# A Fourier filter and a cosine-gated layer on one core: the transforms' inputs split 18 and 20 slots ahead, the filters' rows loaded at the split

## The chip, the cores and the metric

One core of a Trainium2 chip runs the whole computation in one launch. The metric is the device time of that launch in microseconds; lower is better. Several executions of one kernel give a median, and one further execution is recorded by the profiler.

## What is computed

Eight sequences of 3008 tokens with 256 features are filtered in the frequency domain along the sequence; each of the 24064 resulting tokens then goes through two matrix products with a cosine gate between them. Everything is float32.

```python
X = np.fft.rfft(x, axis=1)
y = np.fft.irfft(X * (filt_r + 1j * filt_i)[None], n=3008, axis=1)   # x: 8 x 3008 x 256
h = y.reshape(24064, 256) @ w_in                                     # 256 x 2048
out = (h * np.cos(h)) @ w_out                                        # 2048 x 256
```

## The kernel before

**Split products.** Single precision is kept by writing an operand as a high and a low part in a type that TensorE multiplies at full rate, and by adding three products (high by high, low by high, high by low). A "split" of an operand is thus two instructions: a cast on ACT (the high part) and a subtraction on POOL (the low part). Both are in-order engines, so a split stands in a row with the other work of ACT and POOL.

**The layer.** The tokens are cut into 31 chunks (`SIZES`: 470, 464, then 510 tokens) and a tail that is computed another way. A chunk goes through eight steps, one for each pair of 128-wide blocks of the hidden layer. A step is `hidden` (L698, 12 products on TensorE, "PE" from here on, into `hp`) and the gate: ACT rounds (L708), DVE takes the rest (L709), ACT takes the sine (L712), DVE multiplies (L713), ACT casts to `gh` (L718), POOL subtracts to `gl` (L719). `project` (L733, 12 products that read `gh` and `gl`) follows two steps later (`LAG = 2`).

**The transforms.** Sequence 0 is transformed ahead of the layer. Sequences b = 1 to 7 are transformed underneath it, each as one block of small items strewn between the layer's products: first 16 items of `stage1(b, i)`, then 12 of `stage23(b, i)`. All transformed sequences go through DRAM tensors (`z1`, `z2`) between the stages, and `stage4` brings them back as tokens for later chunks (L543 loads, L555 products).

- `stage1`, b > 1: loads `xf` (L327, issued on SP), splits it into `xh` for each of two halves (L357 on ACT, L358 on POOL, which subtracts in place so that one product carries both parts), multiplies twice (L363), copies out on DVE (L365) and stores (L367, SP).
- `stage23`: loads the filter rows `f` (L375, L376, SP) and the two halves `zf`, `zg` of what stage 1 stored (L385, SP); adds the halves on POOL (L389); splits the sum into `zh` and `zl` (L393 on ACT, L394 on POOL); multiplies three times (L286, L287 read `zh`, L288 reads `zl`); DVE multiplies by the filter rows (L404, L405) and adds (L406); a second split (L409, L410) and three more products follow.

The products of b = 1 in stage 1 need no split, as they run in plain float32 (L336).

**The written order.** Time in the program is counted in slots: 64 slots are 470 tokens of the layer (a step of a 510-token chunk is 8.7 slots). Each part of an item has a due slot, and `run_due` writes the parts between the layer's products when their slot has come. With t for the slot of an item's first product:

```python
step = (end - start - GAP12) / (ones + 2 * n23)
t = start + step * (i - SOON + 1 if b == 1 else 2 * i + 1)
plan(stage1(b, i), t - AHEAD1, [t, t + step][: b], split=t - SPLIT1 if b > 1 else None)
t = start + step * (ones + 2 * i + 2) + GAP12
plan(stage23(b, i), t - AHEAD2, [t, t + GAP23], lambda b=b: len(wrote1.get(b, ())) == 2 * n1, t - SPLIT2)
```

So loads are written `AHEAD` slots ahead of the product and splits `SPLIT` slots ahead. For b > 1, `end - start` is 260 slots, `ones` is 32 and `n23` is 12: an item comes every 2 x (260 - 20) / 56 = 8.57 slots.

From chunk 1 on, PE runs exactly in the written order (`manual_schedule`); ACT, DVE, POOL and the DMA queue of SP are ordered by a scheduler that places instructions by a simulated timeline, with the written order as priority. In chunk 0 the scheduler orders PE too.

**Buffers.** `xh`, `zh` and `zl` share two sets of three buffers (`sh`, `sl`), `f` has three, `xf` three (with the weights' raw tiles), `zf` shares five with the loads of `stage4` (`ld`), and the transforms' products share two banks of PSUM (`ps`).

Of the kernel before, what the change touches and what calls it, by code (L numbers as in the profile page):

```python
# [10 lines left out]
F32 = mybir.dt.float32  # L11
# [10 lines left out]
P = 128  # L22
# [9 lines left out]
APART = 3  # L32
FIRST, LENGTH, BETWEEN = 80, 260, 24
BEFORE, LATER = 140, 28
GAP12, GAP23 = 20, 24
AHEAD1, AHEAD2, AHEAD4 = 28, 28, 24
SPLIT1, SPLIT2 = 10, 12
HALF, WIDE = 252, 512
SIZES = [470] * 4 + [464] + [510] * 26
FROM4, APART4, LATE4, CLOSE4 = 12, 20, 2, 14  # L40
# [137 lines left out]
def fft_filter_then_cos_glu(ctx: ExitStack, tc: tile.TileContext, ins, outT):  # L178
    nc = tc.nc
    x, fa, fb, sgn = ins["x"], ins["fa"], ins["fb"], ins["sgn"]  # L180

    const = ctx.enter_context(tc.tile_pool(name="const", bufs=1))
    fft = ctx.enter_context(tc.tile_pool(name="fft", bufs=2))
# [15 lines left out]
    @contextmanager  # L199
    def behind():  # L200

        if hold:
            with tc.issue_after(hold[0]):
                yield
        else:
            yield

    def load_mats(*names):
        for i, name in enumerate(names):
            rows, cols = ins[name].shape[0], ins[name].shape[1] // 2  # L210
            if i % 2 == 0:
                two = fft.tile([P, 2, 512], F32, name="mats", tag="f", bufs=3)
            raw = two[:, i % 2]
            with tc.issue_after(last_x[0]):
                nc.sync.dma_start(raw[:rows, : 2 * cols], ins[name])
            m = const.tile([P, 2 * cols], F32R, name=name, tag=name)[:rows]
            nc.scalar.copy(m, raw[:rows, : 2 * cols])
            mats[name] = m if name == "m1" else (m[:, :cols], m[:, cols:])
# [65 lines left out]
    def mm3(out, m, hi, lo):  # L284

        nc.tensor.matmul(out, m[0], hi, start=True, stop=False)  # L286
        nc.tensor.matmul(out, m[1], hi, start=False, stop=False)  # L287
        nc.tensor.matmul(out, m[0], lo, start=False, stop=True)  # L288
# [7 lines left out]
    def psum_f(b):  # L296
        if b == 0 and len(done) < 2:
            if not spare:
                spare.extend(ps_h.tile([P, 2, 512], F32, name="hp")[:, u] for u in range(2))
                spare.append(ps_f.tile([P, 512], F32, name="ps", tag="ps"))  # L300
            return spare.pop(0)
        return ps_f.tile([P, 512], F32, name="ps", tag="ps")


    last_x = []
# [63 lines left out]

    def stage23(b, i):  # L370
        piece = slice(i * 512, (i + 1) * 512)
        f = fft.tile([P, 2, 512], F32, name="f", bufs=3)
        fbt, fat = f[:, 0], f[:, 1]
        with tc.issue_after(last_x[0]) if b == 1 else behind():
            nc.sync.dma_start(fbt, fb[:, piece])  # L375
            nc.sync.dma_start(fat, fa[:, piece])  # L376
        zf = fft.tile([P, 512], F32, name="zf", tag="ld", bufs=5)
        assert len(wrote1[b]) == 2 * n1
        if b == 1:
            nc.sync.dma_start(zf, z1s[b].rearrange("n (c k) d -> (n c) (k d)", c=2)[:, piece])  # L380
        else:
            zg = wprep.tile([P, 512], F32, name="zg", tag="t", bufs=5)
            for v, to in enumerate((zf, zg)):
                of = z1s[b].rearrange("n (c v k) d -> (n c) v (k d)", c=2, v=2)[:, v, piece]
                nc.sync.dma_start(to, of)  # L385
        yield
        if b > 1:
            with tc.issue_after(hold[3]):
                nc.gpsimd.tensor_tensor(zf, zf, zg, ALU.add)  # L389
        hi = fft.tile([P, 512], F32R, name="zh", tag="sh", bufs=3)  # L390
        lo = fft.tile([P, 512], F32R, name="zl", tag="sl", bufs=3)
        with tc.issue_after(hold[1]):
            nc.scalar.copy(hi, zf)  # L393
        nc.gpsimd.tensor_tensor(lo, zf, hi.bitcast(F32), ALU.subtract)  # L394
        yield
        ps = psum_f(b)
        mm3(ps, mats["m2"], hi, lo)
        sw = fft.tile([P, 512], F32, name="sw", bufs=2)
        ya = fft.tile([P, 512], F32, name="ya", bufs=2)
        for k in range(2):  # L400
            ks = slice(k * D, (k + 1) * D)
            kc = NK + 2 * i + k
            for to, of in ((slice(0, 64), slice(64, P)), (slice(64, P), slice(0, 64))):
                nc.vector.scalar_tensor_tensor(sw[to, ks], ps[of, ks], sg[of, kc : kc + 1], fbt[of, ks], ALU.mult, ALU.mult)  # L404
        nc.vector.tensor_tensor(ps, ps, fat, ALU.mult)  # L405
        nc.vector.tensor_tensor(ya, ps, sw, ALU.add)  # L406
        yh = fft.tile([P, 512], F32R, name="yh", bufs=2)
        yl = fft.tile([P, 512], F32R, name="yl", bufs=2)
        nc.scalar.copy(yh, ya)  # L409
        nc.gpsimd.tensor_tensor(yl, ya, yh.bitcast(F32), ALU.subtract)  # L410
        yield
        ps = psum_f(b)
        if i == 0:
            mm3(ps[:, :D], mats["m30"], yh[:, :D], yl[:, :D])
            mm3(ps[:, D:], mats["m3"], yh[:, D:], yl[:, D:])
        else:
            mm3(ps, mats["m3"], yh, yl)
        z = fft.tile([P, 512], F32, name="z2t", tag="st", bufs=4)
        nc.scalar.copy(z, ps)
        wrote2.setdefault(b, []).append(i)  # L420
        nc.scalar.dma_start(z2[b * NJ : (b + 1) * NJ].rearrange("j (h c k) d -> (j h c) (k d)", h=2, c=2)[:, piece], z)
# [266 lines left out]
    def hidden(c, s):  # L688
        nt = SIZES[c]
        yh, yl = ys[c]  # L690
        assert filled[c] == nt, (c, filled)
        hp = ps_h.tile([P, 2, 512], F32, name="hp")
        for u in range(2):
            fs = slice(u * P, (u + 1) * P)
            for t in range(NDT):
                for n, (w, y) in enumerate(((0, yh), (0, yl), (1, yh))):
                    with tc.issue_after(last_h[0]) if c == s == 0 else nullcontext():
                        mm = nc.tensor.matmul(hp[:, u, :nt], w_in[s][w][:, t, fs], y[:, t, :nt],  # L698
                                              start=(t == 0 and n == 0), stop=(t == NDT - 1 and n == 2))
                if u == 0 or t == 0:  # L700
                    yield
        last_h[:] = [mm.ins]
        with tc.high_priority() if c == 0 else nullcontext():
            gs[c, s] = gate(hp[:, :, :nt], nt, nc.vector if c == 0 else nc.gpsimd)
# [256 lines left out]
    def convert(g=None, behind=None):  # L961
        with tc.issue_after((behind or hold)[1]), tc.issue_after((behind or hold)[2]):
            if g is None:
                g = prep.pop(0)(None)
                next(g)
            next(g, None)
# [47 lines left out]
    def slot(token):  # L1014
        return SLOTS * NS * token / RUN
# [56 lines left out]
    for k in range(len(steps)):  # L1072
        parts = []
        if k == 2:
            for g in soon[2:]:
                next(g, None)
        if k == 1:
            for g, tie in zip(raws, first_gate):
                convert(g, tie)
        c, s = steps[k]  # L1080
        now_at[0] = c
        if (c, s) == (1, 0):
            fixed.enter_context(tc.manual_schedule(engines={mybir.EngineType.PE}))
        if k < len(steps):
            if s == 6 and c == 0:
                for g in soon:
                    next(g, None)
            if s == 0 and c == 2:
                load_mats("m2", "m3", "m30")
            if s == 0 and c == 3:  # L1090
                load_mats("m1")
            if c == 0:
                while prep and len(prep) > 2 * (NS - 1 - s) - JUST_W:
                    convert()
            parts.append(hidden(c, s))
        if k >= LAG and k < len(steps) - 1:
            parts.append(project(*steps[k - LAG]))
        rate = SIZES[c] / RUN
        now = slot(begins[c]) + SLOTS * rate * s
        for g in parts:  # L1100
            for _ in range(SLOTS // 2):
                run_due(now)
                next(g, None)
                now += rate
# [93 lines left out]
```

## Time and profile before

| what | value |
|---|---|
| median of 3 runs | 2584.69 us (2584.17 to 2585.67) |
| profiled execution | 2588.62 us, its span 2586.8 us |
| PE matmul busy | 2431.1 us, 94% of the span |
| POOL, ACT, DVE busy | 70%, 64%, 63% of the span |
| mean granted TensorE clock | 0.979 |
| moved by DMA | 277.5 MB, mean 107 GB/s |

The profiled execution is 3.9 us above the median and inside one launch, so sums below are made against 2588.62 us. The blocks of the transforms lie between about 195 us and 1820 us of the span; what follows is the tail. "Idle before" is the time in which an engine had nothing running ahead of an instruction, and "waited for" names the instruction of another engine that ended that time. The granted clock is a share of 2.4 GHz; it has two levels, 1.2 and 2.4 GHz, so that a mean of 0.96 over a stretch stands for 8% of it at the lower one.

### The profile page before, as it was taken

Reading aid. Unit: us, or ns where it says so; the run is one execution under the profiler, and the core shown is the slowest. Engines: PE = TensorE matmul, PEld = TensorE weight load, DVE = VectorE, ACT = ScalarE, POOL = GpSimd, SP = SyncE. Lnnn points to the kernel's source line nnn. Section 1 sums busy time; section 2 is a strip of 40 time slices with the busy share of each in tenths; the row PEclk is TensorE's granted clock in tenths of the full one; section 3 lists DMA queues with packets and bytes.
Section 4 is the critical chain, followed back from the end, with each engine's and each line's share of the span. In section 5 each row is a group of like instructions: output and inputs, shape, how many; then the busy total and the mean of one; then the engine's idle time right before and its main releaser. Section 6 shows DMA issues by size and latency. Waiting matters only on the chain. (4 is left out here: it accounts for less than half of the span.)

```text
span 2586.8 us, 35103 instructions
## 1 busy us (share of the span) xinstructions
PE 2431.1 (94%) x12127; PEld 2019.4 (78%) x12127; DVE 1642.0 (63%) x2328; ACT 1663.1 (64%) x2469; POOL 1818.2 (70%) x1465
## 2 busy tenths in 40 slices
PE   7899988999899989999989999889999999999999
PEld 3788866777777768777768777667899999999998
DVE  4836644666566557556745666565577777777776
ACT  4866655667556656665656666555677777777776
POOL 3786666768677768676767777675677777777775
PEclk9999999999999999999989999999999999999999
DMA  8663343544443445445435444343000000000000
GB/s 294 203 210 101 106 129 106 163 136 141 140 145 122 127 130 166 121 118 166 146 103 150 158 134 129 106 149 113 28 20 28 24 28 21 28 20 29 20 17 17
DMA packets 187432, 277.52 MB, mean 107 GB/s; under 512 B 19344, under 2 KB 102480, under 8 KB 187256
## 3 DMA queue, kind: packets, MB, share of 16 engines
q1 hardware_dynamic: 155448, 223.11, 28.8%
q10 hardware_dynamic: 31808, 52.18, 5.6%
q8 instruction: 97, 1.59, 0.3%
q14 instruction: 79, 0.65, 0.1%
HBM read 177.16 MB, written 98.06 MB: 106 GB/s over the span
## 5 line engine op out<-in xcount | busy, mean ns | idle before, releaser
L719 POOL TENSOR_TENSOR gl<-g,gh 128x1020 fp32r<-128x1020 f32 (+2 forms) x240 | 569.1, 2371 | 371.3 <-ACT gh L718 197.6
L698 PE MATMUL hp<-y,w_in 128*128 128x510 f32 (+2 forms) x2976 | 763.7, 397 | 4.3 <-DVE g L713 3.6
L698 PEld LDWEIGHTS hp<-y,w_in 128*128 128x128 f32 x2976 | 575.0, 194 | 128.8 <-issue 7.0
L733 PE MATMUL acc<-gh,w_out 128*128 128x510 f32 (+2 forms) x1984 | 627.1, 398 | 0.0
L709 DVE TENSOR_TENSOR g<-g,hp 128x1020 f32<-128x1020 int32 (+2 forms) x248 | 298.0, 1202 | 272.2 <-ACT g L708 268.1
L733 PEld LDWEIGHTS acc<-gh,w_out 128*128 128x128 f32 x1984 | 374.9, 192 | 77.5 <-issue 3.3
L712 ACT ACTIVATE g<-g,half_pi 128x1020 f32<-128x1020 f32 (+2 forms) x248 | 282.4, 1139 | 187.2 <-DVE g L709 182.8
L733 PE MATMUL acc<-gl,w_out 128*128 128x510 f32 (+2 forms) x992 | 390.4, 395 | 3.1 <-DVE gl L719 2.6
L713 DVE TENSOR_TENSOR g<-g,hp 128x1020 f32<-128x1020 f32 (+2 forms) x248 | 297.5, 1200 | 138.2 <-ACT g L712 136.7
L718 ACT CAST gh<-g 128x1020 fp32r<-128x1020 f32 (+2 forms) x248 | 256.6, 1035 | 173.3 <-DVE g L713 171.9
L708 ACT ACTIVATE g<-hp 128x1020 int32<-128x1020 f32 (+2 forms) x248 | 250.3, 1009 | 159.8 <-PE hp L698 149.6
L358 POOL TENSOR_TENSOR xh<-xf,xh 48x512 fp32r<-48x512 f32 x192 | 243.1, 1285 | 0.0
L404 DVE SCALAR_TENSOR_TENSOR sw<-ps,sg,f 64x256 f32<-64x256 f32 x336 | 162.4, 483 | 120.4 <-PE ps L288 115.8
L761 ACT ACTIVATE qg<-qg,half_pi 128x496 f32<-128x496 f32 (+1 forms) x272 | 187.5, 711 | 70.3 <-DVE qg L760 70.1
L365 DVE COPY z1t<-ps 96x512 f32<-96x512 f32 x192 | 131.6, 685 | 155.6 <-PE ps L363 150.5
L733 PEld LDWEIGHTS acc<-gl,w_out 128*128 128x128 f32 x992 | 190.4, 192 | 44.0 <-DVE gl L719 3.4
L863 PE MATMUL acc<-hg,w_out 128*128 128x496 f32 (+1 forms) x548 | 183.8, 390 | 0.0
L863 PE MATMUL acc<-hgh,w_out 128*128 128x496 f32 (+1 forms) x544 | 182.9, 390 | 0.6 <-POOL hgh L841 0.6
L863 PE MATMUL acc<-hgl,w_out 128*128 128x496 f32 (+1 forms) x540 | 181.3, 390 | 0.0
L410 POOL TENSOR_TENSOR yl<-ya,yh 128x512 fp32r<-128x512 f32 x84 | 108.8, 1296 | 47.6 <-ACT yh L409 47.5
L394 POOL TENSOR_TENSOR zl<-zf,zh 128x512 fp32r<-128x512 f32 x84 | 108.2, 1290 | 40.4 <-ACT zh L393 40.4
L363 PE MATMUL ps<-xh,m 96*96 96x512 f32 x192 | 80.7, 420 | 58.5 <-POOL xh L358 58.1
(162 smaller groups left out, 4193.8 us busy)
## 6 DMA issues: line engine op xcount, KB each, us to landing
xf<-in_x SPq DMA_DIRECT2D x224, 192.0 KB
z<-z1t SPq DMA_DIRECT2D x192, 192.0 KB
z<-z SPq DMA_DIRECT2D x98, 240.0 KB
f<-in_fb SPq DMA_DIRECT2D x84, 256.0 KB
f<-in_fa SPq DMA_DIRECT2D x84, 256.0 KB
zf<-z SPq DMA_DIRECT2D x84, 256.0 KB
z<-z2t ACTq DMA_DIRECT2D x84, 256.0 KB
zg<-z SPq DMA_DIRECT2D x72, 256.0 KB
```

The source lines that it names most:

```text
L358: nc.gpsimd.tensor_tensor(xh[:Q], xf[:Q, v], xh[:Q].bitcast(F32), ALU.subtract)
L404: nc.vector.scalar_tensor_tensor(sw[to, ks], ps[of, ks], sg[of, kc : kc + 1], fbt[of, ks], ALU.mult, ALU.mult)
L698: mm = nc.tensor.matmul(hp[:, u, :nt], w_in[s][w][:, t, fs], y[:, t, :nt], start=(t == 0 and n == 0), stop=(t == NDT - 1 and n == 2))
L708: rounded = nc.scalar.activation(g.bitcast(I32), h, AF.Copy, bias=0.25)
L709: rest = nc.vector.tensor_tensor(g, g.bitcast(I32), h, ALU.subtract)
L712: sine = nc.scalar.activation(g, g, AF.Sin, bias=half_pi, scale=-TWO_PI)
L713: mult = nc.vector.tensor_tensor(g, g, h, ALU.mult)
L718: cast = nc.scalar.copy(gh, g)
L719: lower = engine.tensor_tensor(gl, g, gh.bitcast(F32), ALU.subtract)
L733: nc.tensor.matmul(acc, w_out[s][w][:, u, es], g[:, u], start=(s == 0 and u == 0 and n == 0), stop=(s == NFT // 2 - 1 and u == 1 and n == 2))
L761: nc.scalar.activation(g, g, AF.Sin, bias=half_pi, scale=-TWO_PI)
L863: nc.tensor.matmul(acc, w[a][:, u, e * P : (e + 1) * P], b[:, :, p], start=(q, u, p, n) == (0, 1, 0, 0), stop=(end and p == 1 and n == 2))
```

## The change

The splits of stage 1 are written 18 slots ahead of the first product instead of 10, those of stages 2 and 3 20 slots instead of 12; the loads of `xf` move from 28 to 34 slots ahead, those of `zf` and `zg` from 28 to 36. The gap between the two stages of a block grows from 20 to 28 slots at the same length of a block, so the items come every 8.29 slots instead of 8.57. The loads of the filter rows `f` move from the item's first part (28 slots ahead) to the part with the split (20 slots ahead). PE's written order begins with chunk 2 instead of chunk 1, so the scheduler orders chunk 1 as it does chunk 0.

```diff
-GAP12, GAP23 = 20, 24
-AHEAD1, AHEAD2, AHEAD4 = 28, 28, 24
-SPLIT1, SPLIT2 = 10, 12
+GAP12, GAP23 = 28, 24
+AHEAD1, AHEAD2, AHEAD4 = 34, 36, 24
+SPLIT1, SPLIT2 = 18, 20
...
     def stage23(b, i):
         piece = slice(i * 512, (i + 1) * 512)
-        f = fft.tile([P, 2, 512], F32, name="f", bufs=3)
-        fbt, fat = f[:, 0], f[:, 1]
-        with tc.issue_after(last_x[0]) if b == 1 else behind():
-            nc.sync.dma_start(fbt, fb[:, piece])
-            nc.sync.dma_start(fat, fa[:, piece])
         zf = fft.tile([P, 512], F32, name="zf", tag="ld", bufs=5)
...
         yield
+        f = fft.tile([P, 2, 512], F32, name="f", bufs=3)
+        fbt, fat = f[:, 0], f[:, 1]
+        with tc.issue_after(last_x[0]) if b == 1 else behind():
+            nc.sync.dma_start(fbt, fb[:, piece])
+            nc.sync.dma_start(fat, fa[:, piece])
         if b > 1:
...
-        if (c, s) == (1, 0):
+        if (c, s) == (2, 0):
             fixed.enter_context(tc.manual_schedule(engines={mybir.EngineType.PE}))
```

How this moves instructions is shown at two places.

First, stage 1 of b = 5, item 12, on POOL and on PE. `xh_9625` and `xh_9628` are the two halves that the item's products read, `gl_9616` the gate's low part that stands ahead of them. POOL before, then PE before:

```order
L719 TENSOR_TENSOR gl_9558<-g_9552,gh_9557 128x2x510
L358 TENSOR_TENSOR xh_9575<-xf_9449,xh_9575 48x512
L358 TENSOR_TENSOR xh_9578<-xf_9449,xh_9578 48x512
L719 TENSOR_TENSOR gl_9616<-g_9610,gh_9615 128x2x510
L358 TENSOR_TENSOR xh_9625<-xf_9502,xh_9625 48x512
L358 TENSOR_TENSOR xh_9628<-xf_9502,xh_9628 48x512
```

```order
L698 MATMUL hp_9707<-y0_8840,w_in0_7_94 128x510
L698 MATMUL hp_9707<-y1_8841,w_in0_7_94 128x510
L698 MATMUL hp_9707<-y0_8840,w_in1_7_95 128x510
L363 MATMUL ps_9734<-xh_9628,m1_1919 96x512
L733 MATMUL acc0_9444<-gh_9615,w_out0_5_106 128x510
L733 MATMUL acc0_9444<-gh_9615,w_out1_5_107 128x510
L733 MATMUL acc0_9444<-gl_9616,w_out0_5_106 128x510
```

On POOL `gl_9616` is made ahead of both halves; on PE the products of both halves come ahead of the first product that reads `gl_9616` (that of `xh_9625` 13 rows ahead of it, that of `xh_9628` the 3 rows shown).

The same item now, with `gl_9511` as the gate's part that stands ahead on POOL. POOL now, then PE now:

```order
L719 TENSOR_TENSOR gl_9511<-g_9505,gh_9510 128x2x510
L358 TENSOR_TENSOR xh_9563<-xf_9459,xh_9563 48x512
L358 TENSOR_TENSOR xh_9566<-xf_9459,xh_9566 48x512
L591 TENSOR_TENSOR y1_9309<-y4_9538,y0_9308 128x2x235
L719 TENSOR_TENSOR gl_9581<-g_9575,gh_9580 128x2x510
```

```order
L733 MATMUL acc1_9463<-gl_9511,w_out0_3_102 128x510
L363 MATMUL ps_9654<-xh_9499,m1_1902 96x512
L698 MATMUL hp_9659<-y0_8843,w_in0_6_92 128x510
L698 MATMUL hp_9659<-y1_8844,w_in0_6_92 128x510
L698 MATMUL hp_9659<-y0_8843,w_in1_6_93 128x510
L698 MATMUL hp_9659<-y0_8843,w_in0_6_92 128x510
L698 MATMUL hp_9659<-y1_8844,w_in0_6_92 128x510
L698 MATMUL hp_9659<-y0_8843,w_in1_6_93 128x510
L698 MATMUL hp_9659<-y0_8843,w_in0_6_92 128x510
L698 MATMUL hp_9659<-y1_8844,w_in0_6_92 128x510
L698 MATMUL hp_9659<-y0_8843,w_in1_6_93 128x510
L363 MATMUL ps_9675<-xh_9563,m1_1902 96x512
```

On PE the products that read `gl_9511` now come ahead of the item's first product, by 20 rows from the first of them (the last of them opens the rows shown). Over the whole program, the product of a half `xh` came ahead of the gate's part that precedes it on POOL in 124 of 192 cases, and that of `zl` in 58 of 84; now it is 1 of 192 and 4 of 84. Counted in steps of the layer, a split stood on POOL 1.65 steps ahead of its product in the mean, and stands 2.58 steps ahead now.

Second, the queue of SP in stages 2 and 3 of b = 2 (`z4` is the load of `stage4`). Before, then now:

```order
L543 DMA z4_6190<-z2_112 120x2x256
L375 DMA f_6127<-in_fb 128x512
L376 DMA f_6127<-in_fa 128x512
L385 DMA zg_6352<-z1_4775 128x512
L385 DMA zf_6206<-z1_4775 128x512
L385 DMA zf_6278<-z1_4775 128x512
```

```order
L385 DMA f_6131<-in_fb 128x512
L386 DMA f_6131<-in_fa 128x512
L380 DMA zg_6288<-z1_4749 128x512
L543 DMA z4_6184<-z2_112 120x2x256
L385 DMA f_6207<-in_fb 128x512
L386 DMA f_6207<-in_fa 128x512
```

The loads of `f` still stand among those of `zf`, `zg` and `z4` and still come behind an L543 now and then; the number of L543 rows ahead of them changes by one here. (`f` is loaded by L385 and L386 in the changed kernel, `zf` and `zg` by L380.)

## Rows read from the trace of the kernel before

**Rows 1.** The page's head and part 1: busy time and share by engine.

```profile
span 2586.8 us, 35103 instructions
PE 2431.1 (94%) x12127; PEld 2019.4 (78%) x12127; DVE 1642.0 (63%) x2328; ACT 1663.1 (64%) x2469; POOL 1818.2 (70%) x1465
```

**Rows 2.** Busy time by stretch (us, count): PE, PEld, DVE, ACT, POOL; then clock, DMA share, GB/s.

```profile
195.00:455.00 260.00, 238.30 (x1063) 198.35 (x1062) 150.36 (x198) 156.21 (x212) 166.16 (x109) 0.95 0.37 111
455.00:715.00 260.00, 243.83 (x1073) 195.40 (x1072) 159.14 (x205) 164.11 (x215) 188.38 (x122) 0.98 0.47 143
715.00:975.00 260.00, 234.13 (x1005) 185.34 (x1004) 153.78 (x202) 156.18 (x206) 187.13 (x123) 0.96 0.43 133
975.00:1235.00 260.00, 243.71 (x1082) 196.45 (x1081) 163.89 (x214) 167.52 (x221) 191.36 (x128) 0.99 0.48 145
1235.00:1495.00 260.00, 241.91 (x1039) 193.75 (x1038) 158.71 (x208) 160.15 (x211) 188.03 (x124) 0.96 0.45 137
1495.00:1820.00 325.00, 297.94 (x1318) 238.53 (x1317) 189.10 (x243) 197.56 (x256) 216.19 (x139) 0.97 0.41 125
```

**Rows 3.** Waits of PE between 195 and 1820 us: total, times, longest.

```profile
PE ps L363 <- POOL xh L358: 58.1, 37, 3.9
PE ps L288 <- POOL zl L394: 40.7, 36, 4.2
PE ps L286 <- ACT zh L393: 25.1, 16, 4.3
```

**Rows 4.** Timeline of POOL and of PE, 1145 to 1149 us: start, duration, and idle before.

```profile
1145.16 2.41 POOL L719 TENSOR_TENSOR gl<-g,gh 128x1020 fp32r<-128x1020 f32 x1 [1.60 <-issue]
1147.53 2.52 POOL L358 TENSOR_TENSOR xh<-xf,xh 48x512 fp32r<-48x512 f32 x2
...
1148.86 0.47 PE L363 MATMUL ps<-xh,m 96*96 96x512 f32 x1 [0.96 <-POOL xh L358]
```

**Rows 5.** One early stretch and three without waits of PE, columns as in rows 2.

```profile
325.00:455.00 130.00, 112.02 (x462) 88.59 (x461) 63.20 (x74) 73.61 (x98) 85.66 (x56) 0.92 0.43 119
575.00:640.00 65.00, 64.79 (x295) 52.65 (x294) 39.66 (x46) 46.55 (x64) 52.37 (x35) 1.00 0.50 141
985.00:1050.00 65.00, 65.00 (x295) 53.37 (x294) 50.06 (x73) 45.19 (x61) 53.48 (x36) 1.00 0.51 164
1205.00:1285.00 80.00, 79.82 (x360) 65.28 (x360) 62.59 (x90) 56.75 (x77) 68.45 (x46) 1.00 0.53 167
```

**Rows 6.** Line L363, its instructions: duration ns min/median/max, first and last start us.

```profile
L363 PE MATMUL ps<-xh,m x192: 392/397/740, 328.2 to 1636.5; 96*96 96x512 f32 x192
```

**Rows 7.** Chunk 0 and chunk 1, columns as in rows 2; below, PE's waits in chunk 0.

```profile
60.00:120.00 60.00, 53.07 (x243) 43.62 (x242) 50.12 (x54) 50.76 (x79) 48.39 (x35) 0.97 0.74 235
120.00:195.00 75.00, 75.00 (x344) 61.21 (x343) 31.09 (x33) 52.08 (x73) 59.58 (x60) 1.00 0.57 184
...
PE hp L698 <- DVE g L713: 3.6, 1, 3.6
PE acc L733 <- DVE gl L719: 2.6, 2, 1.3
PE hp L698 <- ACT y L590: 0.7, 1, 0.7
```

**Rows 8.** Waits of POOL between 195 and 1820 us that DMAs ended.

```profile
POOL gl L719 <- DMA xf<-in_x: 19.6, 8, 4.0
POOL gl L719 <- DMA z<-z1t: 18.0, 9, 3.6
POOL gl L719 <- DMA zg<-z: 6.3, 2, 4.9
```

**Rows 9.** Waits of the DMA queue of SP, whole span.

```profile
SPq L543 <- PE ps L555: 612.7, 38, 38.3
SPq L375 <- DVE ps L405: 299.3, 73, 9.0
SPq L327 <- POOL xh L358: 146.2, 42, 18.3
```

## Prediction

> **What bounds the kernel now.** I read the page's shares first, then busy time by stretch, then PE's waits, then the timeline at one of them. PE is busy 94% of the span, and no other engine over 70% [rows 1], so the end is set by PE: by its work, its clock and its gaps. The gaps are where the transforms run. From 195 to 1820 us PE is busy 1499.8 of 1625 us (the sum of the first column of six stretches) at a granted clock of 0.95 to 0.99 [rows 2]. Three waits make up the gap: for `xh` from POOL (58.1 us), for `zl` from POOL (40.7 us) and for `zh` from ACT (25.1 us), 123.9 us in 89 waits, the longest 4.3 us [rows 3]. All three are a split that is not done when its product's turn comes.
>
> The timeline shows why. POOL makes `gl` from 1145.16 to 1147.53 us and then the two halves `xh`; PE came to the product 0.96 us ahead of 1148.86 us, that is at 1147.90 us, when POOL had only just begun on `xh` [rows 4]. POOL is not overloaded there (it was idle for 1.60 us ahead of that `gl`): the split stands behind a `gl` which PE needs only later. This is the order shown for the kernel before, where 182 of the 276 splits' products come on PE ahead of the gate's part that precedes them on POOL.
>
> **The change, part by part.**
>
> *Splits 8 slots earlier.* The first product of stage 1 that needs a split ran at 328.2 us, the last at 1636.5 us [rows 6]; by the planner's formula these are slots 326 and 1879, so a slot is 1308 / 1553 = 0.84 us, and about 0.78 us with the waits taken out. Eight slots are 6.2 to 6.7 us, more than the longest wait of 4.3 us [rows 3]. The order confirms that the move reaches the engines: a split stands 2.58 steps ahead of its product on POOL instead of 1.65. In the place shown, the products that read the preceding `gl` now come 20 PE rows ahead of the item's first product. So whatever is on time for those is on time for the split: `xh` needs 1.26 us more (half of 2.52 us for two) [rows 4], and 20 products take 4.4 us (65 us / 295 = 0.22 us each in a full stretch [rows 5]). I take all 123.9 us away, and bring what may come in its place further down. It cannot be more than that by these rows; at least, if nothing were gained, zero.
>
> *The clock.* Time not granted between 195 and 1820 us, each stretch's length times (1 - clock), is 13.0 + 5.2 + 10.4 + 2.6 + 10.4 + 9.8 = 51.4 us [rows 2], of which PE worked in 92%: 47 us at most. The low clock goes with the gaps: it is 0.92 where PE is busy 112.0 of 130 us, and 1.00 in three stretches in which PE hardly waits [rows 5]. Part of the low time therefore lies in gaps already counted. I take 40 us, between 30 and 47.
>
> *Chunk 1 in the scheduler's order.* In chunk 1 PE is busy 75.00 of 75 us at full clock, so nothing can be gained. In chunk 0, ordered as chunk 1 will be, PE waits 3.6 + 2.6 + 0.7 = 6.9 us [rows 7]. The cost is between 0 and 7 us; I take 4, nearer to chunk 0, the only stretch shown under that ordering.
>
> *Loads.* `zf` and `zg` are read at the split, 16 slots after their load as before (28 - 12, now 36 - 20), and the first of a block still follows the last store of stage 1 by the same slots, since the gap of 28 makes up for the 8: nothing. `xf` has 16 slots to the split instead of 18. POOL's waits that a DMA ended are 43.9 us in 19 [rows 8]; at worst that doubles, and it is hidden as long as POOL has room: its 1137 us between 195 and 1820 us [rows 2] are 70% of 1625 us, and 78% of 1461. If that cover were gone, `gl` behind it would be late and PE with it. `f` has 20 slots to the product, 16 to 17 us. So far its load mostly waited for a buffer (299.3 us in 73 waits for DVE [rows 9]), because three buffers at 8.57 slots give 25.7 slots and it was written 28 ahead; at 20 slots ahead of 24.9 that wait falls away. Nothing on PE, as it hid under SP's own time.
>
> *Denser items.* 8.29 slots instead of 8.57 moves work within a block, and adds none.
>
> *What is late next.* With the splits ready, the next thing that PE can be late for is the gate's `gl` itself. Between 195 and 1820 us no wait of PE for `gl` is among those of weight [rows 3], but its slack is partly the time that PE now waits. The nearest rows are the three stretches where PE runs at full clock with almost no wait while POOL is 81%, 82% and 86% busy [rows 5]; there the gate keeps up with an unstopped PE, in both stages. From them the cost is near 0; from the other side, half of the 123.9 us. I take a tenth, 12 us.
>
> Sum against the profiled execution: 2588.62 - 123.9 - 40 + 4 + 12 = 2440.7 us. That execution is 3.9 us above the median, so I forecast **2437 us**, 5.7% less.
>
> **Rivals.**
>
> *Half of the waits stay.* ACT and POOL are in order: a split written earlier is also earlier in the way of the gate. Where its load or buffer is late, `gh` and `gl` behind it wait, and PE waits for these instead. For it: the loads of `xf` have less time, POOL already waits for DMAs [rows 8], and it gets fuller. Against it: the stretches at full clock [rows 5]. With half of both terms lost, 2588.62 - 82 + 4 - 3.9 = 2507 us. The Trainium skill (TensorE: Matmul & The Clock Gate, on the array's architecture and the engine queue depths) says that ACT, DVE and GpSimd take their instructions strictly first in, first out; the place in rows 4 agrees, as POOL makes the `gl` that PE needs later ahead of the `xh` that PE stands waiting for.
>
> *Buffers bind, and the wait only moves.* `xh`, `zh` and `zl` have three buffers each way. If these were what was short, an earlier split would stand waiting for the product that frees its buffer, and the time would stay: 2585 to 2589 us. Against it: PE's waits end with the split's own work, not with a freed buffer [rows 3, 4]; and a buffer of stage 1 is now held for 18 + 4.1 = 22.1 slots, one of the later stages for little over 20, while three last for 24.9. It fits with 2.8 to 4.9 slots over, so it decides only if ACT runs ahead of PE by more than it does. The Trainium skill (Perfetto Trace Analysis, Optimization Strategy) has the rule that speaks for this rival: the same gap repeating on the engine that should be full can mean too few buffers for the next tile. By that rule the sum would lose both large terms; the releasers in rows 3 and 4 are against it.
>
> *Slower: filter rows come late behind SP's queue.* The queue of SP is in order, and an L543 load has held it for 612.7 / 38 = 16.1 us in the mean and 38.3 us at most [rows 9]. The lead of `f` is now about that mean. If such a wait stood ahead of each load of `f`, it would be issued when its product is due, and its 512 KB at 164 GB/s [rows 5] would land 3.1 us late, 72 times in b = 2 to 7: 225 us, and the time 2440.7 + 225 - 3.9 = 2662 us. It turns the sign from about 148 / 72 = 2.1 us an item. Against it: the longest waits of L543 are for buffers of `stage4` products, the order puts about as many L543 rows ahead of `f` as before, and the loads were issued late before too, when DVE freed the third last buffer, without PE waiting for what DVE makes.
>
> *The change doesn't do what it says.* The scheduler could have left ACT and POOL in their old order. The order shown says otherwise; what could fall flat is that an earlier place means no earlier time. It would read as no change.
>
> **How the numbers follow.** About 0.2% (5 us) is what a measurement of this kernel can tell from no change. The forecast gets 0.68: the cause of the waits is seen and the order removes it. Half staying gets 0.18, since ACT and POOL are in order and SP's waits are long. Buffers binding, or no effect, gets 0.07, of which 0.04 is within 0.2% and the rest a small gain. Late filter rows get 0.07. Faster by over 0.2%: 0.68 + 0.18 + 0.03 = 0.89; within it 0.04; slower 0.07. The forecast's own low end takes all of the waits and of the clock and no new cost, 2588.62 - 123.9 - 47 - 3.9 = 2414 us, and a few us for the rounding of the clock: 2410. Its own high end is about 2475 us. The range reaches into the second case, up to about a third of the gain: 2530 us.
>
> **What would show it.** In the changed kernel's profile, PE's waits for L358, L394 and L393 should fall from 123.9 us to under 20 us; the granted clock under the transforms should read 0.99 or 1.00; POOL's share of the span should rise to about 75%; the transforms should end near 1670 us instead of 1820, with the tail unchanged; SP's wait of the `f` loads for DVE should nearly vanish; in chunk 1 PE should show a few us of waits. It would be wrong if waits of similar total appear on L733 for `gl` or `gh` (the second case), on L357 or L393 for PE (buffers), or on DVE's L404 for a DMA (filter rows).

## The result, and the profile after

The changed kernel takes **2414.59 us** (median; 2412.31 to 2415.47) where the kernel before took 2585.18 us on the same chip: ratio 0.9338, 95% interval [0.9322, 0.9355], 170.6 us or 6.6% less. The profiled execution took 2412.31 us.

Head, part 1 and part 4 of the changed kernel's page, which answer to [rows 1]:

```profile
span 2410.5 us, 35100 instructions
PE 2370.8 (98%) x12127; PEld 2001.0 (83%) x12127; DVE 1640.3 (68%) x2328; ACT 1658.1 (69%) x2469; POOL 1821.8 (76%) x1465
PE 91%; DMA 3%; DVE 2%; POOL 2%; issue 1%; ACT 1%; SPq 0%; ACTq 0%; POOLq 0%; DVEq 0%
```

PE is now busy 98% of the span, and the chain that ended last runs 91% over PE. The work is the same: ACT, DVE and POOL are busy for as long as before, within 5 us each. PE's own busy time fell by 60.3 us for the same 12127 products, which is the first thing to explain. The mean granted clock rose from 0.979 to 0.997.

The stretches, as in [rows 2] (first chunk 1, then the transforms whole, then the first 650 us of the tail):

```profile
120.00:195.00 75.00, 70.55 (x318) 58.71 (x317) 29.19 (x29) 48.38 (x64) 57.78 (x58) 0.98 0.53 169
195.00:1650.00 1455.00, 1447.43 (x6614) 1195.71 (x6613) 978.72 (x1275) 1002.03 (x1326) 1146.43 (x748) 1.00 0.48 147
1650.00:2300.00 650.00, 648.09 (x4198) 590.14 (x4197) 478.91 (x806) 458.45 (x820) 479.39 (x530) 1.00 0.07 24
```

From 195 to 1650 us PE is busy 1447.43 of 1455 us at full clock. What took 1625 us takes 1455, so the whole gain lies under the transforms; the tail is unchanged (648.09 of 650 us, and before, from 1820 to 2470 us, also 648.09). What PE still waits for between 195 and 1650 us, against [rows 3]:

```profile
PE ps L286 <- DVE ya L406: 3.7, 4, 1.2
PE ps L288 <- POOL zl L394: 3.5, 2, 2.3
PE ps L363 <- POOL xh L358: 0.2, 1, 0.2
```

The waits for a split went from 123.9 us in 89 to 3.7 us in 3. The wait of 3.7 us for `ya`, DVE's product with the filter rows, was 0.4 us before: under the transforms it is all that came in their place. One more wait is new; it stands in chunk 1, for the tokens that `stage4` loads:

```profile
PE ps L555 <- DMA z<-z: 4.5, 1, 4.5
```

**What a wait costs beside its idle time.** One wait of the kernel before, on PE's timeline (start, duration, and idle before):

```profile
1133.46 0.39 PE L733 MATMUL acc<-gl,w_out 128*128 128x510 f32 x1
1134.88 0.47 PE L363 MATMUL ps<-xh,m 96*96 96x512 f32 x1 [1.04 <-POOL xh L358]
1135.19 0.62 PE L733 MATMUL acc<-gh,w_out 128*128 128x510 f32 x2
```

And three products in a row of the changed kernel:

```profile
1153.27 0.40 PE L733 MATMUL acc<-gl,w_out 128*128 128x510 f32 x1
1153.50 0.40 PE L286 MATMUL ps<-zh,m 128*128 128x512 f32 x1
1153.74 0.39 PE L287 MATMUL ps<-zh,m 128*128 128x512 f32 x1
```

Unhindered, products start 0.23 to 0.24 us apart although each is recorded with 0.4 us: they overlap. At the wait the next one started 1.42 us later, 1.19 us more than 0.23; the idle time counts from the recorded end, so the view says 1.04. The product behind the wait then held the next one for 0.31 us instead of 0.24. Together 1.26 us were lost, 0.22 us more than the wait's row tells, and this part is entered as PE's busy time. Taken 89 times it would be 20 us, an estimate from this one place.

The rest of the 60.3 us is the clock. The last lines of two views, over all stretches that the trace has at the lower clock level, before and now:

```profile
sum 109.25, PE 90.15 PEld 69.52 DVE 53.83 ACT 32.05 POOL 72.10; mean PE 3.76 PEld 2.90 DVE 2.24 ACT 1.34 POOL 3.00
sum 13.64, PE 10.09 PEld 7.18 DVE 4.55 ACT 5.52 POOL 6.39; mean PE 3.36 PEld 2.39 DVE 1.52 ACT 1.84 POOL 2.13
```

PE was busy for 90.15 us at the lower level and is busy for 10.09 us there now. Products of L698 start 0.425 us apart at that level and 0.228 us at the upper one (medians), so the lower level made PE's work 42 us longer before and 5 us now. That is 37 us of the 60.3, or 40 us if a product is taken to last twice as long. The other 20 to 23 us come to 0.24 to 0.27 us for each of the 86 waits for splits that went, near the 0.22 us of the place shown. The same sum for half the move and for either stage alone (runs below) gives 0.24 to 0.29 us a wait. It isn't a price of every gap: in the kernel with the copies alone, 26 waits for `ya` left nothing of the kind.

### The profile page after: what moved, and what is told of

Its sections match the earlier page's. It is cut to its first block, busy times and chain, and to the rows that moved or that the text cites. A ratio compares the mean times of both kernels' runs of the same rounds, so it can differ in the third digit from the quotient of the medians.

```text
span 2410.5 us, 35100 instructions
## 1 busy us (share of the span) xinstructions
PE 2370.8 (98%) x12127; PEld 2001.0 (83%) x12127; DVE 1640.3 (68%) x2328; ACT 1658.1 (69%) x2469; POOL 1821.8 (76%) x1465
## 4 chain that ended last, share of the span: by engine, by line
PE 91%; DMA 3%; DVE 2%; POOL 2%; issue 1%; ACT 1%; SPq 0%; ACTq 0%; POOLq 0%; DVEq 0%
PE hp L698 26%; PE acc L733 26%; PE acc L863 15%; PE x L779 8%; PE w L779 4%; PE ps L555 4%; PE ps L779 2%; PE ps L363 2%; PE ps L286 2%; PE ps L288 2%; PE ps L287 2%; POOL gl L719 1%; DMA ff<-in_fa 1%; DVE sw L404 0%; DVE g L713 0%
## 5 line engine op out<-in xcount | busy, mean ns | idle before, releaser
L698 PE MATMUL hp<-y,w_in 128*128 128x510 f32 (+2 forms) x2976 | 744.6, 390 | 4.3 <-DVE g L713 3.6
L698 PEld LDWEIGHTS hp<-y,w_in 128*128 128x128 f32 x2976 | 559.4, 189 | 125.9 <-issue 6.2
L733 PE MATMUL acc<-gh,w_out 128*128 128x510 f32 (+2 forms) x1984 | 614.6, 392 | 0.0
L733 PEld LDWEIGHTS acc<-gh,w_out 128*128 128x128 f32 x1984 | 368.9, 188 | 76.2 <-issue 1.8
L733 PE MATMUL acc<-gl,w_out 128*128 128x510 f32 (+2 forms) x992 | 384.0, 389 | 0.5 <-POOL gl L719 0.5
L718 ACT CAST gh<-g 128x1020 fp32r<-128x1020 f32 (+2 forms) x248 | 256.9, 1036 | 121.7 <-DVE g L713 120.2
L785 ACT COPY sum<-x 128x496 f32<-128x496 f32 (+1 forms) x136 | 78.5, 577 | 63.7 <-PE x L779 63.4
L779 PE MATMUL x<-diff,sum 128*128 128x248 f32 (+1 forms) x816 | 115.9, 278 | 0.0
```

The lines of the kernel that those rows point to most:

```text
L718: cast = nc.scalar.copy(gh, g)
L733: nc.tensor.matmul(acc, w_out[s][w][:, u, es], g[:, u], start=(s == 0 and u == 0 and n == 0), stop=(s == NFT // 2 - 1 and u == 1 and n == 2))
L779: nc.tensor.matmul(bank[:, p * n : (p + 1) * n], ws[a], y[b], start=first and p == i == 0, stop=last and i == 2, skip_group_check=True)
```

## The experiments

Each is told against the changed kernel or the kernel before, as its diff says. None leaves out a part of the computation.

### Which part of the change carries the gain

The changed kernel once more, on the chip of three runs below (stages 2 and 3 alone, the copies alone, the best version):

> The changed kernel itself, on the same chip as the three that follow, to compare them with. 2410 to 2417 us.

2414.8 us against 2587.49 before, 0.933 [0.9317, 0.9343].

**The written order alone**, against the kernel before:

```diff
-        if (c, s) == (1, 0):
+        if (c, s) == (2, 0):
```

> The kernel before with one line changed: TensorE's written order begins with chunk 2. Theory (the gain is the place of the splits on ACT and POOL): no part in the gain; chunk 0 loses its two waits for gl (2.6 us) and chunk 1 gains one for a load of stage4 (about 4.5 us), so 2583 to 2590 us and PE still waits about 124 us for the splits. Rival (the free order lets the scheduler set up a better start for the blocks that follow): at least 20 us faster, 2565 us or less.

2582.97 us against 2586.78, 0.9987 [0.9978, 0.9996]: 3.8 us or 0.13% less, under the 0.2% that the prediction counts as no change, and the three waits stay (56.3, 40.3 and 23.6 us). The new wait in chunk 1 is 6.3 us, and for `gh`, not for a load. **The changed kernel with the order of chunk 1 written again** (the same line back to `(1, 0)`):

> The changed kernel with TensorE in the written order from chunk 1 again. Theory: within 5 us of the changed kernel (2410 to 2420 us), the 4.5 us wait for the load of stage4 in chunk 1 gone and two waits for gl of about 1.3 us back in chunk 0. Rival as above: at least 20 us slower, 2435 us or more.

2411.25 us, 0.932 [0.9308, 0.9332]. The wait for L555 is gone, and chunk 1 is full again:

```profile
120.00:195.00 75.00, 75.00 (x344) 61.27 (x343) 31.15 (x34) 51.33 (x71) 58.96 (x59) 1.00 0.57 184
```

It is 3.3 us below the changed kernel, which its interval alone doesn't separate from nothing; a second pair below gives 3.7 us with the same sign. Both pairs compare runs on different chips. So this part of the change gains nothing with early splits and rather costs 3 to 4 us. Why the same line took 3.8 us off ahead of late splits no run shows.

**The filter rows' load back in the first part**, 36 slots ahead (the five lines of `f` in `stage23` moved back up, all else as changed):

> The changed kernel with the filter rows' load back in the item's first part, now 36 slots ahead. Three buffers release it at the same point either way, and the scheduler issues it when a buffer is free. Theory: no effect, 2410 to 2420 us. Rival (the gain came from the queue of SP, which the early loads of filter rows used to hold up): most of the gain is lost, 2500 us or more, and SP waits longer for DVE.

2414.28 us, 0.933 [0.9318, 0.9342]: nothing. Two rows of SP's queue waits say why, first the changed kernel's, then this one's:

```profile
SPq L385 <- DVE ps L405: 229.8, 72, 9.7
```

```profile
SPq L375 <- DVE ps L405: 230.2, 72, 9.7
```

The load waits for the same buffer as long, whichever part it is written in. So the scheduler goes by when one of three buffers comes free, and the written place doesn't decide.

**Loads early, splits late**, against the changed kernel: every load and the gap stay as changed, the splits go back, and the filter rows keep their 20 slots in a part of their own.

```diff
-SPLIT1, SPLIT2 = 18, 20
+SPLIT1, SPLIT2 = 10, 12
+ROWS2 = 20
...
             nc.sync.dma_start(fat, fa[:, piece])
+        yield
...
             plan(stage23(b, i), t - AHEAD2, [t, t + GAP23], lambda b=b: len(wrote1.get(b, ())) == 2 * n1, t - SPLIT2)
+            due.append([t - ROWS2, False, due[-1][2], due[-1][3]])
```

> The changed kernel with the splits back at 10 and 12 slots; all loads stay early (34, 36 and 20 slots), as do the gap of 28 and the order of chunk 1. Theory: nearly all of the gain is lost, 2540 to 2590 us, with 90 to 125 us of waits of PE for the splits; what is gained is only the few first items of a block that waited for their loads. Rival (the gain came from earlier loads and a freer queue of SP): the gain stays, 2450 us or less.

2578.67 us, 0.9965 [0.9954, 0.9977]. PE's waits between 195 and 1840 us (lines shifted by one or two):

```profile
PE ps L364 <- POOL xh L359: 69.6, 42, 3.9
PE ps L289 <- POOL zl L396: 33.0, 23, 3.7
PE ps L287 <- ACT zh L395: 11.0, 10, 2.6
```

113.6 us of the 123.9 are back, and with them all of the gain but about 9 us. The splits' place carries it, and the loads, the gap and the items' spacing alone do not. Whether early splits would do without the earlier loads no run tells.

### How far ahead is enough

**Half way**, against the changed kernel:

```diff
-GAP12, GAP23 = 28, 24
-AHEAD1, AHEAD2, AHEAD4 = 34, 36, 24
-SPLIT1, SPLIT2 = 18, 20
+GAP12, GAP23 = 24, 24
+AHEAD1, AHEAD2, AHEAD4 = 31, 32, 24
+SPLIT1, SPLIT2 = 14, 16
```

> The changed kernel with half the move: splits 14 and 16 slots ahead, loads 31 and 32, gap 24. In the order, 63 of 276 products still come on PE ahead of the gate's part that precedes their split on POOL (182 before, 5 after). Theory in its first form (time alone: every wait shrinks by 4 slots, 3.2 us, and the longest was 4.3): nearly the whole gain, 2415 to 2425 us. In its second form (the order against the gate's part decides, and waits go with the number of such cases, 63 / 182 of 124 us): 35 to 50 us of waits left and 2460 to 2490 us.

2485.37 us, 0.9604 [0.959, 0.9619], and over the whole span:

```profile
PE ps L288 <- POOL zl L394: 24.6, 9, 4.9
PE ps L363 <- POOL xh L358: 23.9, 17, 3.1
...
PE ps L286 <- ACT zh L393: 4.6, 5, 1.8
```

Four slots are 3.1 to 3.4 us by the prediction's slot, more than most of the waits of before; by lead alone nearly all should have gone. 53.1 us stayed. In this kernel 49 of 192 products of `xh` and 14 of 84 of `zl` still come on PE ahead of the `gl` that precedes their split on POOL (before 124 and 58, after 1 and 4). So the first form in the expectation fell. The second held for the time (2485 us in 2460 to 2490), but its 35 to 50 us of waits lie a little under the 53.1 us measured. By stage the count fits stage 1 (49 / 124 of 58.1 us is 23.0, and 23.9 stayed) and not the later ones (14 / 58 of 65.8 us is 15.9, and 29.2 stayed).

The traces show the link directly when each split is matched with its products in order of time. In the kernel before, every wait for `xh`, `zh` or `zl` falls on one of the 182 items of the count (77 of them wait for over 0.1 us), and none on the other 94. Half way, all but one of 0.4 us fall on the 63. So the count says which items can wait, and roughly how much waiting there is; by the mean lead alone nearly all of it would have gone half way.

**Two slots more** (`GAP12` 30, `AHEAD1, AHEAD2` 36 and 38, `SPLIT1, SPLIT2` 20 and 22):

> The changed kernel with the splits two slots further ahead: 20 and 22, loads 36 and 38, gap 30. A buffer is then held 24.1 slots where three last 24.6. Theory: the waits for the splits are gone already, so the same as the changed kernel within 5 us, 2410 to 2420 us. Rival (buffers bind): ACT's casts of splits wait for products on PE, gates behind them are late and PE waits for gl or gh; slower than the changed kernel by 15 us or more.

2410.4 us, 0.9315 [0.9301, 0.9329], 4 us less. One wait of PE for a split is left, of 0.3 us, and none for a buffer: a split of stage 1 now holds its buffer for 20 + 4.1 = 24.1 slots, while by the prediction's count three buffers last 3 x 8.2 = 24.6. The rival of the buffers costs nothing even here. But POOL begins to wait for products of stage 1, between 195 and 1650 us:

```profile
POOL gl L719 <- PE ps L363: 14.9, 6, 3.6
```

This row was 5.4 us in 2 waits in the changed kernel, and there was none before. Whether it is a buffer that comes free late, the row doesn't say; none of it reaches PE.

### Each stage by itself

Stage 1's splits alone, against the kernel before:

```diff
-AHEAD1, AHEAD2, AHEAD4 = 28, 28, 24
-SPLIT1, SPLIT2 = 10, 12
+AHEAD1, AHEAD2, AHEAD4 = 34, 28, 24
+SPLIT1, SPLIT2 = 18, 12
```

> The kernel before with stage 1 alone changed: its splits 18 slots ahead, xf 34. Theory: the wait for xh (58.1 us in the profile) goes, those for zl and zh (65.8 us) stay. Each us of wait has cost about 170.6 / 123.9 = 1.38 us with the clock, so 2585 - 80 = 2505 us (2490 to 2520). Rival (what is freed in one stage comes back in the next, since ACT and POOL have a fixed pace): above 2545 us, with the waits for zl and zh grown.

2486.73 us, 0.9612 [0.9598, 0.9626], 3 us under the range expected. And stages 2 and 3 alone, against the changed kernel (with the order of chunk 1 written):

```diff
-AHEAD1, AHEAD2, AHEAD4 = 34, 36, 24
-SPLIT1, SPLIT2 = 18, 20
+AHEAD1, AHEAD2, AHEAD4 = 28, 36, 24
+SPLIT1, SPLIT2 = 10, 20
...
-        if (c, s) == (2, 0):
+        if (c, s) == (1, 0):
```

> The counterpart of e8: the changed kernel with stage 1 as before (splits 10, loads 28 slots ahead) and the written order from chunk 1; splits of stages 2 and 3 stay 20 ahead. If the two stages' waits add up: e8 gained 100 of 172 us, so this gains about 72: 2510 to 2520 us, with about 60 us of waits for xh left and under 10 for zl and zh. If each stage's stalls set up the other's: the two gains don't add to 172, and the time is outside 2495 to 2535 us.

2503.6 us, 0.9677 [0.9663, 0.969], 6 us under the forecast for gains that add, but not outside 2495 to 2535 us, where gains that don't add would lie. PE's waits of stage 1 alone, then of stages 2 and 3 alone, over the whole span:

```profile
PE ps L288 <- POOL zl L394: 32.0, 37, 3.2
PE ps L286 <- ACT zh L393: 18.0, 15, 2.9
```

```profile
PE ps L363 <- POOL xh L358: 68.0, 42, 3.9
...
PE ps L286 <- DVE ya L406: 3.9, 5, 1.2
...
PE ps L288 <- POOL zl L394: 3.5, 2, 2.3
```

Each early split ends its own waits and leaves the other's. The gains are about 100 and 84 us, 184 together against 173 for both, so they nearly add. They don't follow exactly from the rows of before, since what stays changes too: 50.0 us are left of 65.8 in the one, 68.0 where 58.1 stood in the other.

### The slower rival: filter rows that come late

**Loaded behind the split**, against the changed kernel: the load of `f` is written after the split, and behind a DVE copy from `zl` into `f`, so that it can't be issued before the split is done.

```diff
-        f = fft.tile([P, 2, 512], F32, name="f", bufs=3)
-        fbt, fat = f[:, 0], f[:, 1]
-        with tc.issue_after(last_x[0]) if b == 1 else behind():
-            nc.sync.dma_start(fbt, fb[:, piece])
-            nc.sync.dma_start(fat, fa[:, piece])
...
         nc.gpsimd.tensor_tensor(lo, zf, hi.bitcast(F32), ALU.subtract)
+        f = fft.tile([P, 2, 512], F32, name="f", bufs=3)
+        fbt, fat = f[:, 0], f[:, 1]
+        nc.vector.tensor_copy(f[:, :, :1], lo[:, :2].bitcast(F32).rearrange("p (a n) -> p a n", a=2))
+        with tc.issue_after(last_x[0]) if b == 1 else behind():
+            nc.sync.dma_start(fbt, fb[:, piece])
+            nc.sync.dma_start(fat, fa[:, piece])
```

> The changed kernel with the load of the filter rows made to depend on the finished split of the same item (DVE copies one column of zl into the rows first), so that it starts some 6 us ahead of the product instead of about 16, and DVE has 84 small copies more that wait for POOL. It measures from which lead the filter rows count. If 6 us are still enough (512 KB land in about 3 us, the queue of SP is mostly free): 2412 to 2425 us. If a load behind a held queue of SP is late (the slower rival of the prediction): DVE waits for the DMA of f, and the time is 2450 us or more.

2490.09 us, 0.9621 [0.9605, 0.9637], 75 us above the changed kernel. PE's longest waits, then the one of DVE for a load:

```profile
PE ps L286 <- DVE ya L407: 41.7, 23, 4.0
PE ps L556 <- DVE ya L407: 9.9, 4, 3.5
```

```profile
DVE sw L405 <- DMA f<-in_fb: 26.5, 19, 3.3
```

This kernel adds 84 copies as well as lateness. **The copies alone**, into a tile that nothing else uses, with the loads free:

```diff
         nc.gpsimd.tensor_tensor(lo, zf, hi.bitcast(F32), ALU.subtract)
+        nc.vector.tensor_copy(spot, lo[:, :2].bitcast(F32))
         yield
...
+    spot = const.tile([P, 2], F32, name="spot")
```

> The changed kernel with the 84 small DVE copies of e7, into a spot of their own, so that the loads of the filter rows are free of them. What e7 lost (75 us) was either the rows' lateness or the copies. If the lateness: 2412 to 2425 us here, no wait of DVE for a DMA. If the copies, which took DVE 1.15 us each in the median there: 2470 us or more.

2466.94 us, 0.9532 [0.9519, 0.9545], 52 us above the changed kernel, with no wait of DVE for the rows; it is in neither range expected, 3 us under that of the copies. So of the 75 us the copies make 52, and by difference the lateness some 23, if the copies cost as much in both. The rival's mechanism is real, and cheaper than its price of 225 us; in the changed kernel it doesn't occur at all, as no wait of DVE for a load of `f` is in its trace.

Why copies of two columns cost so much is on the timeline of POOL and DVE, 704 to 714 us:

```profile
705.53 2.38 POOL L721 TENSOR_TENSOR gl<-g,gh 128x1020 fp32r<-128x1020 f32 x1
706.89 1.05 DVE L395 COPY spot<-zl 128x2 f32<-128x2 f32 x1
...
712.56 1.22 POOL L593 TENSOR_TENSOR y<-y,y 128x470 fp32r<-128x470 f32 x1
712.64 1.16 DVE L395 COPY spot<-zl 128x2 f32<-128x2 f32 x1 [0.64 <-POOL zl L394]
```

`gl` ends at 707.91 us and the first copy at 707.94; `y` ends at 713.78 and the second at 713.80. Of the 84 copies 12 began with POOL between instructions and took 0.15 to 0.17 us. The other 72 began beside a running POOL instruction, and all end within 0.1 us of the end of one: 68 with the one that was running, three that began in its last 0.1 us with the next, and one, of 4.1 us, with the third.

```profile
L395 DVE COPY spot<-zl x84: 154/1208/4100, 202.8 to 1637.5; 128x2 f32<-128x2 f32 x84
```

A copy thus waits for POOL to finish, and the gate and `ya` wait behind it on DVE: the copies held DVE for 98.5 us in all, while DVE stood idle for `zl` ahead of them for only 6.7 us. The Trainium skill (SBUF — State Buffer, on its two separate sides) says that DVE in its two-port modes and GpSimd share one port pair, which whoever starts first holds for the whole instruction. The 72 copies agree with it.

### The best version

The numbers of two slots more, and the order of chunk 1 written:

```diff
-GAP12, GAP23 = 28, 24
-AHEAD1, AHEAD2, AHEAD4 = 34, 36, 24
-SPLIT1, SPLIT2 = 18, 20
+GAP12, GAP23 = 30, 24
+AHEAD1, AHEAD2, AHEAD4 = 36, 38, 24
+SPLIT1, SPLIT2 = 20, 22
...
-        if (c, s) == (2, 0):
+        if (c, s) == (1, 0):
```

> The two small gains together: splits 20 and 22 slots ahead (2410.4 us alone) and TensorE's written order from chunk 1 (2411.3 us alone). Theory: they act in different places (the transforms' blocks, and chunk 1), so they add: 2404 to 2409 us, no waits of PE left between 120 and 195 us and under 5 us of waits after it. Rival: either was the spread between chips and runs, and this one stands at 2410 to 2415 us as the changed kernel does.

**2406.67 us** (2406.35 to 2406.74), 0.9298 [0.9286, 0.9311], 8.1 us below the changed kernel on the same chip. It is the fastest of all, and 3.7 us below the same numbers without the written chunk 1.

## Why the prediction was right, and by how much it was off

The sign, the mechanism and the range held; 2437 us forecast is 22 us too high. The measured time lies near the range's low end, and nearly on the 2414 us of its sum by chance: that sum has 7 to 10 us too much of the clock and nothing for the restart below. Profiled execution against profiled execution, 176.3 us went (2588.62 to 2412.31) where the sum had 147.9.

- **Waits, 123.9 us taken away**: 120.2 went. That the order on POOL and ACT against `gl` is the cause is shown by loads without splits (113.6 us stay) and by the half way (53.1 us stay; the count of 63 inverted cases gives 43), and all waits of before lie on inverted cases.
- **What is late next, 12 us**: 3.7 us, for `ya` and not for `gl`. The tenth that was taken was too much; the three full stretches [rows 5] would have given near 0.
- **The clock, 40 us**: the lower level took 42 to 45 us of PE's work before and takes 5 now, 37 to 40 us less. Right, within its bounds of 30 to 47.
- **Chunk 1, 4 us**: the one wait there is 4.5 us; the two waits for `gl` in chunk 0 (2.6 us, [rows 7]) went at the same time, and the two pairs of runs put the whole at 3 to 4 us. Ahead of late splits the same line gained 3.8 us, so this term holds for the changed kernel alone.
- **The step that was missing** is the mechanism of the restart: the sum took a wait at its idle time alone. PE's busy time fell by 60.3 us, 37 to 40 of which are the clock; the other 20 to 23 us, against the 20 estimated above from one wait, are products that ran on alone before a gap and started slowly behind it. With the clock at 40 us and the restart at 20, 4.6 us from waits and late next and 2 from the first chunks make up 27 of the 28.4 us. That the 20 us go with the waits is shown by four kernels with 0.24 to 0.29 us a wait; what PE does in that time is read from the one place.
- **Loads of `f`**: that SP's wait of these loads for DVE would nearly vanish was wrong: 299.3 us in 73 waits [rows 9] became 229.8 in 72. The step counted 20 slots of lead against 24.9 of buffer, as if the written place set the time of issue; the run with the rows 36 slots ahead shows that it doesn't. It cost nothing, as said.
- The other signs held: POOL at 76% (about 75 forecast), the clock at 1.00, the transforms' end near 1650 us (1670), the same tail.
- **Rivals**: half of the waits staying is what the half way did (2485 us; the rival's 2507), not the change. Buffers cost PE nothing even two slots further out, though POOL then waits more. Late filter rows exist only where they are made late.

## What to carry to other kernels

When PE waits for short work on an in-order engine, look at what stands ahead of that work on its queue and count how often PE needs it before that neighbour's result: the count, not the mean lead, said about how much a shift would bring. Price a short wait at more than its idle time: against the kernel before, each microsecond of split waits taken away came with 170.6 / 120.2 = 1.42 us in the change, 101.3 / 70.8 = 1.43 half way, and 100.0 / 73.9 = 1.35 and 83.9 / 52.4 = 1.60 with either stage alone. Where a scheduler orders a DMA queue, a buffer's release can set when a load is issued, and moving its line then changes nothing.

## What was not expected of the hardware

A DVE copy of 128 x 2 elements took 1.21 us in the median and 0.15 us at the least, since it ended with a POOL instruction beside it in 72 of 84 cases; 84 of them cost the kernel 52 us. And a gap of about 1 us on PE cost 0.22 us beyond its idle time, besides the low clock that went with the gaps (PE was busy for 90.15 us at the lower level before, and for 10.09 after).
